# Attention and FFN block on one core: a new model for the order of TensorE's and ScalarE's work, transposes of o and of the FFN input by DMA, q and k in one padded tile

## The chip, the core and the metric

The program runs on one core of one Trainium2 chip. The core has a matrix engine (TensorE; its weight loads are listed apart), VectorE (DVE), ScalarE (ACT), GpSimd (POOL) and SyncE (SP), which here issues every DMA. The metric is the device time of one execution in microseconds. Lower is better.

## The reference

The input x has 2048 rows of 576 columns. A transformer block is computed: h = x + Attention(layernorm(x)), then out = h + FFN(layernorm(h)). Attention has 32 heads of 18 columns and works on four segments of 512 rows, with a memory M and its normalizer z that grow from segment to segment:

```python
for s in range(N):
    logits = jnp.einsum('bhqd,bhkd->bhqk', qs, ks) * scale + mask
    p = _softmax(logits, axis=-1)
    a_dot = jnp.einsum('bhqk,bhkd->bhqd', p, vs)
    pq = phi(qs)
    a_mem = (pq @ M) / (pq @ z + 1e-06)
    o = g * a_mem + (1.0 - g) * a_dot
    M = M + phi(ks).T @ vs
    z = z + phi(ks).sum(rows)
```

Here phi(t) is t + 1 above zero and exp(t) below, g is the sigmoid of beta for each head, the mask is causal within a segment, and o is multiplied by wo. The FFN is gelu(x w1 + b1) w2 + b2 with 4608 inner columns.

## The kernel before, in words

The work is cut into Python generators ("threads"), five kinds for each segment s of 512 rows (four tiles of 128):

- P (line 193): layernorm of x, TensorE transposes (`transposes5`, line 165) with a ScalarE copy out of PSUM, then q, k and v, each in two halves of five matmuls (`proj_half`, line 171). q and k go into tiles where each head's 18 columns are padded to 32 (`q_pad`, `k_pad`), and from there to memory (`qd`, `kd`, lines 232 and 238). For segments 0 to 2, phi(k) is then written over `k_pad` in place (line 245).
- M (line 253): phi(k) times v, added up in `MZacc`.
- A (line 283): attention, in eight groups of four heads. `fetch` (line 288) reads q and k of a group back from memory, transposed by two DMAs (lines 292 and 294). Two groups make five steps (STEPS, line 280), so a segment has 20: score matmuls into `st` (four PSUM banks, one buffer; line 372), Exp on ScalarE (line 376), the mask on GpSimd (line 378), and the products with v into `ox` (one buffer; line 346). `memory` adds the memory's part, `combine` normalizes and writes o into `o_nat`. phi(q) takes ScalarE, GpSimd and DVE (lines 301 to 306).
- B (line 407): TensorE transposes of o, times wo, plus x, layernorm (line 428), h to memory (`hd`), TensorE transposes of the normed h into `xn2T_s`.
- C (line 463): FFN1 in 36 chunks of five matmuls with 512 columns (lines 488 and 489), the copy to `hT` by DVE (line 490), a Gelu in place over twelve chunks at a time on ScalarE (line 495), so three for each segment; then FFN2, eight groups of 36 matmuls (line 511). The bias b1 is a 65th row of the last block of w1, loaded by a DMA of its own (line 475).

A loop at line 566 builds the order. Each generator yields a cost on TensorE and a delay; the loop keeps a clock of TensorE (and a rough one of ScalarE, `on_act`), takes the first thread of the list that is ready, in the order A, P and M, B, C, and emits its next piece. `manual_schedule` keeps that order for TensorE and ScalarE. `hT` lies in the space of the early tiles, so C0 comes after P3. What a thread has to wait for is in its `add` call:

```python
add(f"A{s}", thread_A(s), f"P{s}", *([f"M{s - 1}", f"A{s - 1}"] if s else []), *([f"B{s - 2}"] if s > 1 else []))
add(f"B{s}", thread_B(s), f"A{s}", *([f"B{s - 1}"] if s else []), *([f"C{s - 3}"] if s > 2 else []))
add(f"C{s}", thread_C(s), f"B{s}", f"P{NSEG - 1}", *([f"C{s - 1}"] if s else []))
```

All other PSUM work shares three banks (`bank`, line 162), taken in turn.

Of the kernel before, what the change touches and what calls it, by code (L numbers as in the profile page):

```python
# [16 lines left out]
def kernel(  # L17
# [15 lines left out]
    nc = tc.nc  # L33
# [21 lines left out]
    xtp = ctx.enter_context(tc.tile_pool(name="xtp", bufs=2))  # L55
    xn2Tp = ctx.enter_context(tc.tile_pool(name="xn2Tp", bufs=3))
# [6 lines left out]
    w1pool = ctx.enter_context(tc.tile_pool(name="w1pool", bufs=3))  # L63
# [11 lines left out]
    x_pre = []  # L75
    wts = {}

    def load_w(nm, W, wt):
        nc.sync.dma_start(out=wt[:, 0:4, :], in_=W[0:512, :].rearrange("(k p) n -> p k n", p=P))
        nc.sync.dma_start(out=wt[0:64, 4, :], in_=W[512:576, :])  # L80
        nc.gpsimd.memset(wt[64:KTAIL, 4, :], 0.0)
        wts[nm] = wt

    for tl in range(TPS):
        xt = xpool.tile([P, D], BF16, tag="x", name="xt")
        nc.sync.dma_start(out=xt[:], in_=x[tl * P:(tl + 1) * P, :])
# [12 lines left out]
    xn_bufs = [early([P, XW], f"xn{j}") for j in range(2)]
# [30 lines left out]
    b1_row = B_b1.rearrange("(o f) -> o f", o=1)  # L130
# [12 lines left out]
    qd = [tc.dram_tile([L, H * 32], BF16, name=f"qd{j}") for j in range(NSEG)]  # L143
    kd = [tc.dram_tile([L, H * 32], BF16, name=f"kd{j}") for j in range(NSEG)]
    hd = tc.dram_tile([S, D], F32, name="hd")
    big = {}
    w2_sb = const.tile([P, NF, D], BF16, name="w2_sb")
    w2v = B_w2.rearrange("(f p) d -> p f d", p=P)

    def layernorm(src, xn):  # L150
        stats = small.tile([P, 2, 6], F32, tag="stats", name="stats")
        for c in range(2):
# [4 lines left out]
        nc.vector.tensor_scalar(out=rstd[:], in0=mv[:, 1:2], scalar1=EPS, scalar2=None, op0=ALU.add)  # L157
        nc.gpsimd.tensor_tensor(out=rstd[:], in0=rstd[:], in1=mhalf[:], op=ALU.pow)  # L158
        nc.vector.tensor_scalar(out=xn[:, 0:D], in0=src, scalar1=mv[:, 0:1], scalar2=rstd[:],  # L159
                                op0=ALU.subtract, op1=ALU.mult)  # L160

    def bank(name):
        return psC.tile([P, 512], F32, tag="c", name=name)

    def transposes5(src):
        pt = bank("ps_t")[:].bitcast(BF16)[:, 0:KT * P].rearrange("p (k q) -> p k q", q=P)
        for k in range(KT):
            nc.tensor.transpose(out=pt[:, k, :], in_=src[:, k * P:(k + 1) * P], identity=ident[:])  # L168
        return pt

    def proj_half(xT_t, wt, hf, name):
        ps = bank(name)
        for k in range(4):
            nc.tensor.matmul(out=ps[:, 0:HALF], lhsT=xT_t[:, k, :], rhs=wt[:, k, hf * HALF:(hf + 1) * HALF],  # L174
                             start=(k == 0), stop=False)
        nc.tensor.matmul(out=ps[:, 0:HALF], lhsT=xT_t[0:KTAIL, 4, :], rhs=wt[0:KTAIL, 4, hf * HALF:(hf + 1) * HALF],
                         start=False, stop=True)
        return ps[:, 0:HALF]
# [4 lines left out]
    class Clock:  # L183
        pe = 0.0
        act = 0.0

    clk = Clock()

    def on_act(cost):
        clk.act = max(clk.act, clk.pe) + cost  # L190
        return clk.act

    def thread_P(s):
        va = v_augs[s]
        xns, xnTs = {}, {}

        def load(tl):
            t = s * TPS + tl
            if s == 0:
                xt = x_pre[tl]  # L200
            else:
                xt = xpool.tile([P, D], BF16, tag="x", name="xt")
                nc.sync.dma_start(out=xt[:], in_=x[t * P:(t + 1) * P, :])
            xns[tl] = xn_bufs[tl % 2]
            layernorm(xt[:], xns[tl])

        def flip(tl):
            pt = transposes5(xns[tl])
            xnTs[tl] = xtp.tile([P, KT, P], BF16, tag="xnT", name="xnT_t")
            nc.scalar.copy(out=xnTs[tl][:], in_=pt)  # L210
            on_act(0.65)

        load(0)
        load(1)
        yield 0.0, 3.0
        flip(0)
        yield 0.28, 0.0
# [398 lines left out]
```

## Time and profile before

| what | value |
|---|---|
| median of 3 runs | 573.83 us (571.47 to 577.94) |
| profiled execution | 574.9 us, its span 573.2 us |
| mean granted TensorE clock | 0.932 of full speed |
| TensorE, DVE, ScalarE, GpSimd busy | 500.0, 302.2, 292.3, 148.6 us |
| DMA | 63.42 MB, mean 111 GB/s |

All times of the rows below are microseconds from the start of the span. A row of a table of windows has the window, its length, the busy time of TensorE, its weight loads, DVE, ScalarE and GpSimd (in brackets how many instructions began there), then the granted TensorE clock as a share of full speed, the DMA share and GB/s. In a list of groups the columns are busy time and mean time of one in ns, then the idle time before them and what ended most of it. In the chain each row is start, length, and what ran or what was waited for. A letter q behind an engine's name (SPq) is its instruction queue.

### The profile page before, as it was taken

Reading aid. Unit: us, or ns where it says so; the run is one execution under the profiler, and the core shown is the slowest. Engines: PE = TensorE matmul, PEld = TensorE weight load, DVE = VectorE, ACT = ScalarE, POOL = GpSimd, SP = SyncE. Lnnn points to the kernel's source line nnn. Section 1 sums busy time; section 2 is a strip of 40 time slices with the busy share of each in tenths; the row PEclk is TensorE's granted clock in tenths of the full one; section 3 lists DMA queues with packets and bytes.
Section 4 is the critical chain, followed back from the end, with each engine's and each line's share of the span. In section 5 each row is a group of like instructions: output and inputs, shape, how many; then the busy total and the mean of one; then the engine's idle time right before and its main releaser. Section 6 shows DMA issues by size and latency. Waiting matters only on the chain.

```text
span 573.2 us, 11399 instructions
## 1 busy us (share of the span) xinstructions
PE 500.0 (87%) x4709; PEld 317.4 (55%) x4736; DVE 302.2 (53%) x722; ACT 292.3 (51%) x223; POOL 148.6 (26%) x236
## 2 busy tenths in 40 slices
PE   3756869878768997979989979799999999999997
PEld 2544656656544444647755534477754477644675
DVE  5384755656766766824437867144486611366200
ACT  2224666846766784776654768955415330033300
POOL 5013543514364303513332531132131000000000
PEclk9886977978977997979999999999999999999999
DMA  8977633515343442512233543211235421242020
GB/s 256 352 214 197 184 78 93 146 55 131 115 114 91 121 134 82 171 33 71 81 70 112 145 131 125 70 41 33 63 106 160 149 73 32 79 149 84 0 63 22
DMA packets 80347, 63.42 MB, mean 111 GB/s; under 512 B 38148, under 2 KB 72104, under 8 KB 80296
## 3 DMA queue, kind: packets, MB, share of 16 engines
q1 hardware_dynamic: 80296, 62.70, 37.2%
q8 instruction: 37, 0.61, 0.4%
q14 instruction: 14, 0.11, 0.1%
HBM read 38.83 MB, written 15.47 MB: 95 GB/s over the span
## 4 chain that ended last, share of the span: by engine, by line
PE 65%; ACT 12%; DVE 8%; DMA 5%; issue 4%; POOL 3%; SPq 2%; ACTq 0%; DVEq 0%; POOLq 0%
ACT hT L495 6%; ACT pt L376 4%; PE ox L346 4%; PE st L372 3%; PE ps_k L174 2%; DMA xt<-in_A_x_dram 2%; PE ps_q L174 2%; PE ps_v L174 2%; DVE stats L153 2%; PE ps_o L174 1%; POOL pt L378 1%; PE ps_t L168 1%; DMA kd_212<-k_pad_132 1%; POOL rstd L158 1%; DVE hT L490 1%
## 5 line engine op out<-in xcount | busy, mean ns | idle before, releaser
L376 ACT ACTIVATE pt<-st 128x2048 bf16<-128x2048 f32 x80 | 150.1, 1876 | 82.6 <-PE st L372 70.7
L511 PEld LDWEIGHTS <-hT 128*128 128x128 bf16 x1152 | 110.2, 99 | 34.2 <-issue 4.6
L378 POOL TENSOR_SCALAR_AFFINE_SELECT pt<-pt 128x512 bf16<-128x512 bf16 x128 | 82.8, 664 | 139.2 <-ACT pt L376 139.1
L495 ACT ACTIVATE hT<-hT 128x6144 bf16<-128x6144 bf16 x12 | 63.9, 5324 | 75.1 <-DVE hT L490 75.0
L488 PEld LDWEIGHTS <-w1g 128*128 128x128 bf16 x576 | 53.8, 98 | 67.6 <-issue 11.8
L346 PEld LDWEIGHTS <-pt 128*128 128x128 bf16 x1280 | 43.3, 98 | 21.9 <-POOL pt L378 11.2
L174 PEld LDWEIGHTS <-xnT_t 128*128 128x128 bf16 x384 | 38.0, 106 | 27.7 <-issue 13.7
L372 PE MATMUL st<-QT,KTt 32*128 32x384 bf16 (+3 forms) x512 | 34.4, 323 | 19.1 <-ACT pt L376 16.5
L306 DVE SCALAR_TENSOR_TENSOR pq<-e_g,r_g 128x512 bf16<-128x512 bf16 x24 | 17.6, 734 | 30.1 <-ACT e_g L301 25.3
L372 PEld LDWEIGHTS <-KTt 32*128 32x128 bf16 x512 | 10.0, 93 | 41.2 <-issue 37.6
L304 POOL TENSOR_SCALAR r_g<-QT 128x512 bf16<-128x512 bf16 x24 | 14.7, 612 | 60.3 <-DVE pq L306 54.8
L158 POOL TENSOR_TENSOR rstd<-rstd,mhalf 128x1 f32<-128x1 f32 x32 | 17.6, 558 | 48.2 <-DVE rstd L157 44.5
L174 PE MATMUL ps_k<-wt_k,xnT_t 128*128 128x288 bf16 x128 | 24.9, 326 | 4.8 <-ACT xnT_t L210 2.9
L174 PE MATMUL ps_o<-wt_o,oT_t 128*128 128x288 bf16 x128 | 22.7, 306 | 5.3 <-ACT oT_t L416 2.6
L174 PE MATMUL ps_q<-wt_q,xnT_t 128*128 128x288 bf16 x128 | 25.2, 330 | 2.3 <-ACT xnT_t L210 1.2
L489 PEld LDWEIGHTS <-w1g 65*128 65x128 bf16 x144 | 14.1, 98 | 17.6 <-issue 0.7
L174 PE MATMUL ps_v<-wt_v,xnT_t 128*128 128x288 bf16 x128 | 22.1, 299 | 2.1 <-DVE k_pad_133 L236 1.6
L434 ACT COPY xn2T_s<-ps_t 128x640 bf16<-128x640 bf16 x16 | 10.9, 690 | 23.6 <-PE ps_t L168 23.6
L429 POOL TENSOR_TENSOR h_t<-h_t,b_bc 128x576 f32<-128x576 f32 x16 | 20.4, 1274 | 8.9 <-DVE xn_1_155 L159 4.6
L416 ACT COPY oT_t<-ps_t 128x640 bf16<-128x640 bf16 x16 | 10.6, 691 | 20.6 <-PE ps_t L168 20.6
L153 DVE BATCH_NORM_STATS2 stats<-xt 128x6 f32<-128x288 bf16 x32 | 13.3, 440 | 12.4 <-DMA xt<-in_A_x_dram 12.3
L174 PEld LDWEIGHTS <-oT_t 128*128 128x128 bf16 x128 | 12.6, 103 | 11.0 <-issue 3.5
(864 smaller groups left out, 927.6 us busy)
## 6 DMA issues: line engine op xcount, KB each, us to landing
w1g<-in_B_w_dram SPq DMA_DIRECT2D x36, 512.0 KB
w_sb<-in_B_w_dram SPq DMA_DIRECT2D x4, 1296.0 KB
hd<-h_t SPq DMA_DIRECT2D x16, 288.0 KB
hc<-hd SPq DMA_DIRECT2D x16, 288.0 KB
xt<-in_A_x_dram SPq DMA_DIRECT2D x16, 144.0 KB
w1g<-in_B_w_dram SPq DMA_DIRECT2D x36, 64.0 KB
out_dram<-ot SPq DMA_DIRECT2D x16, 144.0 KB
wt_q<-in_A_wq_dram SPq DMA_DIRECT2D x1, 576.0 KB
```

Source lines behind the costliest of these rows:

```text
L153: nc.vector.bn_stats(out=stats[:, c, :], in_=src[:, c * HALF:(c + 1) * HALF])
L158: nc.gpsimd.tensor_tensor(out=rstd[:], in0=rstd[:], in1=mhalf[:], op=ALU.pow)
L174: nc.tensor.matmul(out=ps[:, 0:HALF], lhsT=xT_t[:, k, :], rhs=wt[:, k, hf * HALF:(hf + 1) * HALF], start=(k == 0), stop=False)
L306: nc.vector.scalar_tensor_tensor(out=pq[:], in0=e_g[:], scalar=1.0, in1=r_g[:], op0=ALU.min, op1=ALU.add)
L346: nc.tensor.matmul(out=banks[g][:, qt, i, :], lhsT=src, rhs=va[kt][:, 4 * g + i, :], start=fresh, stop=False, skip_group_check=True)
L372: nc.tensor.matmul(out=st[:, i, off:off + n], lhsT=kts[g][rows, kt * P:(kt + 1) * P], rhs=qts[g][rows, kt * P:L], start=True, stop=True, t ...
L376: nc.scalar.activation(out=pt_[:], in_=st[:], func=ACT.Exp, scale=scale)
L378: nc.gpsimd.affine_select(out=pt_[:, :, off:off + P], in_=pt_[:, :, off:off + P], pattern=[[0, 4], [1, P]], compare_op=ALU.is_ge, fill=0.0 ...
L429: nc.gpsimd.tensor_tensor(out=h_t[:], in0=h_t[:], in1=b2_bc[:], op=ALU.add)
L488: nc.tensor.matmul(out=ps[:], lhsT=w1g[:, k, j * P:(j + 1) * P], rhs=xn2T_s[:, k, :], start=(k == 0), stop=False)
L495: nc.scalar.activation(out=hT[:, f0:f1, :], in_=hT[:, f0:f1, :], func=ACT.Gelu_apprx_tanh)
L511: nc.tensor.matmul(out=ps[:, 0:HALF], lhsT=hT[:, f, tl * P:(tl + 1) * P], rhs=w2_sb[:, f, hf * HALF:(hf + 1) * HALF], start=(f == 0), stop ...
```

## The change

The loop now keeps a time for each of TensorE, ScalarE, DVE, GpSimd and SP (`free`, `on`) and for each of the three shared PSUM banks (`banks_free`). A thread yields a time at which it is ready and the number of banks that it needs, and is taken when both are there. The list is now in the order B, A, then X, P, M, then C. Layernorm and transposes of x become a thread X of their own. In the code:

```diff
+    free = dict(pe=0.0, act=0.0, dve=0.0, pool=0.0, sp=0.0)
+    def on(eng, cost, *after):
+        end = max([free[eng]] + [a + SEM for a in after]) + cost
+        free[eng] = end
+        return end
...
+    def flip_dma(dst, src, t0, cost=1.25):
+        nc.sync.dma_start_transpose(out=dst, in_=src)
+        return on("sp", cost, t0) + 2.0
+    def copy(out, in_, t0, ca, cd):
+        if max(free["act"], t0) + ca < max(free["dve"], t0) + cd:
+            nc.scalar.copy(out=out, in_=in_)
+            return on("act", ca, t0)
+        nc.vector.tensor_copy(out=out, in_=in_)
+        return on("dve", cd, t0)
...
     for s in range(NSEG):
-        add(f"A{s}", thread_A(s), f"P{s}", *([f"M{s - 1}", f"A{s - 1}"] if s else []), *([f"B{s - 2}"] if s > 1 else []))
+        add(f"B{s}", thread_B(s), f"A{s}", *([f"B{s - 1}"] if s else []), *([f"C{s - 2}:0"] if s > 1 else []))
+    for s in range(NSEG):
+        add(f"A{s}", thread_A(s), f"P{s}", *([f"M{s - 1}", f"A{s - 1}"] if s else []), *([f"B{s - 1}"] if s > 1 else []))
+    for s in range(NSEG):
+        add(f"X{s}", thread_X(s), *([f"X{s - 1}", f"P{s - 1}:0"] if s else []), *([f"P{s - 3}"] if s > 2 else []))
+        add(f"P{s}", thread_P(s), *([f"P{s - 1}"] if s else []), *([f"M{s - 2}"] if s > 1 else []))
...
+            def at(t):
+                return max(t.ready, bank_at(t.banks))
+            pick = next((t for t in open_ if at(t) <= free["pe"] + 1e-6), None)
```

q and k of a tile go into one padded tile (two of them in turn), in the order k, q, then v, with one write to memory, and a group's q and k come back by one transposing DMA of 256 columns. phi(k) goes to five tiles of its own:

```diff
+    pads = [early([P, G, 2, 4, 32], f"qk_pad{j}") for j in range(2)]
+    fk_pads = [early([P, H, 32], f"fk_pad{j}") for j in range(NK)]
...
+        qk = alp.tile([P, 2, L], BF16, tag="qk", name="qk")
+        at = flip_dma(qk[:], qkd[s][:, g * 256:(g + 1) * 256], qk_at[s], 2.1)
```

o goes to memory in five chunks of 128 columns, each when the heads in it are done, and comes back transposed; so does the normed h. The TensorE transposes and ScalarE copies of both are gone (those of x stay):

```diff
+            for k in ready_chunks.get(g, []):
+                nc.sync.dma_start(out=od[s].rearrange("(t p) c -> p t c", p=P)[:, :, k * P:(k + 1) * P],
+                                  in_=o_nat[:, :, k * P:(k + 1) * P])
...
+                oT_at[s] = flip_dma(oTs[s][:, k:k + 1, :], od[s][:, k * P:(k + 1) * P], wr)
...
+        for k in range(KT):
+            x2_at[s] = flip_dma(x2T[:, k:k + 1, :], x2d[s][:, k * P:(k + 1) * P], wr)
```

In segments 1 to 3 the last step of the layernorm of x is done by GpSimd. The bias b1 is loaded once, transposed, and added when FFN1 leaves PSUM; once all of attention is done, ScalarE takes FFN1 out of PSUM with Gelu and bias in one instruction a chunk:

```diff
+                if f"A{NSEG - 1}" in done and not pend:
+                    nc.scalar.activation(out=hT[:, f, :], in_=ps[:], func=ACT.Gelu_apprx_tanh, bias=b1c[:, f:f + 1])
+                    act_at[f] = banks_free[b] = on("act", 0.65, t1)
+                    continue
+                nc.vector.tensor_scalar(out=hT[:, f, :], in0=ps[:], scalar1=b1c[:, f:f + 1], scalar2=None, op0=ALU.add)
```

FFN2 is emitted in pieces of six matmuls instead of eight or nine. w1 has three fixed buffers, w2 is loaded in six parts instead of four, most memsets move behind the first layernorm, and the first loads are x, wk, x, wq, wv.

## Rows read from the trace of the kernel before

**Rows 1.** The page, part 1: busy time, share, instructions of each engine.

```profile
PE 500.0 (87%) x4709; PEld 317.4 (55%) x4736; DVE 302.2 (53%) x722; ACT 292.3 (51%) x223; POOL 148.6 (26%) x236
```

**Rows 2.** Table of windows, cut at the stages of the program.

```profile
40.80:120.60 79.80, 63.41 (x802) 44.54 (x803) 46.34 (x129) 52.32 (x53) 32.59 (x51) 0.80 0.49 133
120.60:175.50 54.90, 41.60 (x509) 28.45 (x508) 35.19 (x96) 36.35 (x39) 23.33 (x34) 0.84 0.40 107
175.50:252.30 76.80, 68.22 (x592) 35.96 (x600) 49.25 (x105) 54.93 (x36) 23.07 (x34) 0.92 0.40 114
252.30:295.00 42.70, 42.70 (x545) 30.62 (x542) 17.22 (x47) 24.63 (x17) 15.73 (x25) 0.94 0.23 57
295.00:370.20 75.20, 64.50 (x573) 34.40 (x579) 47.76 (x101) 54.21 (x35) 21.93 (x32) 0.98 0.41 119
370.20:406.70 36.50, 36.50 (x478) 26.56 (x476) 14.36 (x40) 21.76 (x14) 11.29 (x19) 0.95 0.16 45
406.70:465.50 58.80, 57.15 (x354) 31.92 (x358) 36.41 (x70) 22.69 (x12) 8.49 (x10) 1.00 0.38 119
...
495.10:570.00 74.90, 74.21 (x464) 45.33 (x466) 28.69 (x45) 15.97 (x3) 0.00 (x0) 1.00 0.22 68
```

**Rows 3.** The chain that ended last, in order of time: segment 0, and the end.

```profile
16.11 6.82 DMA kd_212<-k_pad_132
23.06 0.77 DVE k_pad_132 L245
...
31.94 3.49 DMA qd_208<-q_pad_131
35.45 1.23 SPq L292
...
39.31 1.26 SPq L294
...
565.44 4.42 PE ps_f_7412 L511 x36
```

**Rows 4.** Groups of instructions, costliest first.

```profile
L376 ACT ACTIVATE pt<-st 128x2048 bf16<-128x2048 f32 x80 | 150.1, 1876 | 82.6 <-PE st L372 70.7 <-POOL pt L378 9.3 <-POOL r_g L304 2.5
...
L495 ACT ACTIVATE hT<-hT 128x6144 bf16<-128x6144 bf16 x12 | 63.9, 5324 | 75.1 <-DVE hT L490 75.0
...
L158 POOL TENSOR_TENSOR rstd<-rstd,mhalf 128x1 f32<-128x1 f32 x32 | 17.6, 558 | 48.2 <-DVE rstd L157 44.5 <-DMA xt_6252<-in_A_x_dram 3.6
...
L153 DVE BATCH_NORM_STATS2 stats<-h_t 128x6 f32<-128x288 f32 x32 | 14.1, 453 | 0.6
...
L495 ACT ACT_TABLE_LOAD x7 | 9.0, 1283 | 0.1
...
L159 DVE TENSOR_SCALAR xn_1_155<-h_t,mv,rstd 128x576 bf16<-128x576 f32 x8 | 5.2, 653 | 4.2 <-POOL rstd L158 4.2
```

**Rows 5.** TensorE's instructions in order of time: values, transposes, scores.

```profile
45.13 0.63 PE L346 MATMUL ox<-v_aug_0_138,pt 128*128 128x19 bf16 x16
...
123.15 0.56 PE L168 MATMUL ps_t<-ident,o_nat_156 128*128 128x128 bf16 x7 [2.04 <-DVE o_nat_156 L331]
...
127.81 0.39 PE L372 MATMUL st<-QT,KTt 32*128 32x512 bf16 x4
```

**Rows 6.** ScalarE's instructions in order of time, FFN2 of segment 0.

```profile
268.75 1.88 ACT L376 ACTIVATE pt<-st 128x2048 bf16<-128x2048 f32 x1 [1.57 <-PE st L372]
...
285.35 1.88 ACT L376 ACTIVATE pt<-st 128x2048 bf16<-128x2048 f32 x1 [1.57 <-PE st L372]
```

**Rows 7.** ScalarE's instructions in order of time, A1 up to the first FFN matmul.

```profile
128.32 1.88 ACT L376 ACTIVATE pt<-st 128x2048 bf16<-128x2048 f32 x1 [1.33 <-PE st L372]
...
174.45 1.88 ACT L376 ACTIVATE pt<-st 128x2048 bf16<-128x2048 f32 x1 [0.80 <-POOL pt L378]
```

**Rows 8.** Line 490, the copy of an FFN1 chunk out of PSUM (min/median/max ns).

```profile
L490 DVE CAST hT<-ps_f_2736 x1: 692/692/692, 179.7 to 179.7; 128x512 bf16<-128x512 f32 x1
```

**Rows 9.** Instructions in order of time, first 60 us, SP's queue.

```profile
9.98 1.77 SPq L563 DMA_DIRECT2D w_sb<-in_B_w_dram  x2
```

More of the change, by code (lines that the diff above doesn't have):

```diff
@@ L157, in layernorm @@
         nc.vector.tensor_scalar(out=rstd[:], in0=mv[:, 1:2], scalar1=EPS, scalar2=None, op0=ALU.add)
+        t1 = on("dve", 1.25, t0)
         nc.gpsimd.tensor_tensor(out=rstd[:], in0=rstd[:], in1=mhalf[:], op=ALU.pow)
[L159 to L169, printed above, removed]
@@ L171, in proj_half @@
-    def proj_half(xT_t, wt, hf, name):
-        ps = bank(name)
-        for k in range(4):
[L174 to L178, printed above, removed]
+        t1 = on("pool", 0.56, t1)
+        eng = nc.vector if apply == "dve" else nc.gpsimd
@@ L187, with thread_X, fetch, ask @@
[L187 to L191, printed above, removed]
+    xnTs, xn_at = {}, {}
+    def thread_X(s):
+        yield 0.0, 0
+        xnTs[s] = xTp.tile([P, KT, L], BF16, tag="xT", name="xnT")
+        xs = {}
+        def fetch(tl):
+            xs[tl] = x_pre[tl] if s == 0 else load_x(s * TPS + tl)
+            return dma(free["pe"], 2.5)
+        at = [4.0, 4.5, 7.0, 7.5] if s == 0 else [0.0] * TPS
+        def ask(tl):
+            if tl < TPS:
+                t1 = fetch(tl)
+                at[tl] = max(at[tl], t1)
+        ask(0)
+        ask(1)
+        for tl in range(TPS):
+            ask(tl + 2)
+            done = layernorm(xs[tl][:], xn_bufs[tl % 2], at[tl], "pool" if s else "dve")
+            if s == 0 and tl == 0:
+                make_identity(nc, ident[:])
+            yield done + SEM, 1
+            pt, j = bank("ps_t")
+            pt = pt[:].bitcast(BF16)[:, 0:KT * P].rearrange("p (k q) -> p k q", q=P)
+            for k in range(KT):
+                nc.tensor.transpose(out=pt[:, k, :], in_=xn_bufs[tl % 2][:, k * P:(k + 1) * P], identity=ident[:])
+            t1 = on_pe(0.3)
+            banks_free[j] = copy(xnTs[s][:, :, tl * P:(tl + 1) * P], pt, t1, 0.69, 0.8)
+            xn_at[(s, tl)] = banks_free[j]
+            if s == 0 and tl == 0:
+                pads_first()
+            yield 0.0, 0
@@ L193, in thread_P @@
+    qk_at = {}
     def thread_P(s):
         va = v_augs[s]
[L195 to L211, printed above, removed]
@@ L354, in thread_A, with drain @@
-        yield 0.0, 5.0
+                    combine(g, oxs[g], free["pe"])
+        yield qk_at[s], 0
+        fetch(s, 2)
         phi(0)
         phi(1)
-        prev, late, ready = None, [], 0.0
+        prev, late, st_at = None, [], 0.0
+        def drain(prev):
+            psi, pgp, todo, at = prev
+            if s and psi in (0, 3):
+                g = 2 * pgp + (psi == 3)
+                yield max(pq_at[g] + SEM, mem_at[s - 1] + SEM), 1
+                memory(g)
+            fresh = todo[0][0] not in oxs
+            yield max(at + SEM, ox_at[0] + SEM if fresh else 0.0), 0
+            values(todo)
+            if psi == 0:
+                flip_o()
@@ L569 @@
             if pick is None:
[L570 to L575 removed]
+                pick = min(open_, key=at)
+                free["pe"] = at(pick)
+            try:
+                pick.ready, pick.banks = next(pick.gen)
+                done.add(pick.name + ":0")
             except StopIteration:
[L577 removed]
+                threads.remove(pick)
```

456 lines of the change are left out of this document (233 added, 223 removed).

## The prediction

> **What bounds the kernel now.** I read the page's busy line first, then a table of windows cut at the events of the program, then the chain that ended last, and last the order of single instructions around the waits that the chain named.
>
> TensorE is busy 500 of 573.2 us [rows 1], and no other engine is above 302 us. So the question is where TensorE loses time. The table by stage [rows 2] answers it. Its cuts are: 9.4 first matmul, 40.8 first score matmul of segment 0, 120.6 first transpose of that segment's attention output o, 175.5 first FFN matmul, and from there the alternation of FFN1 and FFN2. In the last line, the last segment's FFN alone, TensorE is busy 74.21 of 74.9 us at clock 1.00: nothing is to be had there. In 40.8 to 175.5 it is busy 63.41 of 79.80 and 41.60 of 54.90 us, and at a granted clock of 0.80 and 0.84, that is, about a third or more of these stretches at the lower of its two levels (1.2 GHz) after gaps. This is the finding: for 175.5 us no FFN work exists. FFN needs B0 (output projection, layernorm, transposes of segment 0) and P3 (the last of the projections), and B0 comes late: A0 ends at 120.6 and B0 needs another 55 us, because its pieces stand behind A1 and P3 in the list of threads.
>
> After 175.5 the FFN fills TensorE, yet not fully: 68.22 of 76.80, 64.50 of 75.20, 57.15 of 58.80 and 74.21 of 74.90 us are busy, which leaves 21.6 us idle; and the clocks of 0.92, 0.94, 0.98 and 0.95 mean that 16, 12, 4 and 10% of these stretches ran at half speed, some 12.3, 5.1, 3.0 and 3.7 us, half of which, 12 us, is lost [rows 2]. Together 33.6 us.
>
> **The sum that I forecast.** The end is S, the time of the first FFN matmul, plus R, what TensorE still has to do after it, plus the tail. Before: S = 175.5, R = 570.0 - 175.5 = 394.5, tail 573.2 - 570.0 = 3.2.
>
> *Start of A0.* Before, it begins at 40.8. In the chain [rows 3] one write of k takes 6.82 us to land, and the operation that overwrites this same tile with phi(k) waits for it (23.06), then the scalar queue behind it, then TensorE. The change gives phi(k) tiles of its own, so this wait goes. It comes back in part: q and k share two padded tiles, so a tile's k copy waits for the write of two tiles ago; I take half the loss, some 1.5 of 3 us. Next, the fetch: the chain shows transposed loads at 1.23 to 1.26 us each, and A0 starts when four of them are through (35.45 to 40.6). After, one load brings q and k of a group. A load of twice the columns appears nowhere in the trace; it lies between 1.25 us (the issue is the cost) and 2.5 us (the bytes are), and I take 2.1, nearer the upper end since the shown loads move the same bytes in each instruction. That saves about 3 us net of the landing. Memsets behind the first square root and the order of weight loads may give another us or cost one. A0 starts at 36 (34 to 41).
>
> *A0.* It has 20 steps: scores, Exp of 2048 columns, mask, value products. The Exp takes 1.876 us [rows 4] and waits for its scores, since there is one score buffer: no step can be under 1.88 + 0.39 (score group, [rows 5]) = 2.3 us. Before, 79.8 us for A0 is 4.0 a step. Where only FFN2 pieces lie between, five steps from 268.75 to 285.35 took 3.3 each, the two phi operations included [rows 6]. The new order, which books each engine and bank, should hold 3.3 where the old one let copies of P stand before the Exp: 20 x 3.3 = 66, so A0 ends at 102 (82 to 121).
>
> *B0.* TensorE transposes and ScalarE copies go; o goes to memory and comes back transposed. New on the path: the write's landing, 3 us (3.49 and 6.82 in [rows 3]; o is written while little else moves), two transposed loads, 2.5, and landing, 1.5. The three earlier chunks lie behind A0's steps. Then four tiles of projection, add and layernorm. By [rows 4] a tile's statistics are 2 x 0.45, the power on GpSimd 0.56 and the scaling 0.65 us; with two adds and the small operations 3 us a tile, 12 in all. Then the write, 3, five loads, 6.3, and landing, 1.5. Sum 30 us (25 if loads overlap, 52 if B keeps the 54.9 us of before). B now heads the list, so A1 yields to it. S = 36 + 66 + 30 = 132.
>
> What must be done by then besides: P1 to P3 are 36 units of q, k or v tile projections. TensorE has 96 us for these, A0, and part of A1; before, it did them, A0 and most of B0 in 105 busy us, at the lower clock in part. It fits, barely; if P3 is late S moves with it.
>
> *R.* Transposes that go: 24 groups of five after 175.5. Seven in a row took 0.56 us [rows 5], with 0.22 for the latency of one, hence 0.057 each and 0.28 a group: -6.7 us. Steps that come on top: in the old order, 13 steps of A1 were through by 175.5 (first and last in [rows 7]); now A1 starts at 104 and by 132 has some 8. Five more steps, each 0.39 of scores and sixteen value products at (0.63 - 0.17)/15 = 0.031, 0.9 us: +4.5. Of the 33.6 us of idle and half clock I give half back, -17: a wait that is booked is filled with FFN pieces, but each FFN1 group still frees its bank by a DVE or ScalarE operation. That gives R = 394.5 - 6.7 + 4.5 - 17 = 375 (359 with all of it, 392 with none).
>
> *What costs nothing.* The bias moves from a row of the weights to the eviction: 0.692 us before [rows 8], with a scalar operand between 0.69 and, as bounded by twice that, 1.4; I take 0.7 since size and operands in PSUM are the same. It hides behind a chunk's TensorE time, (74.9 - 8 x 4.42)/36 = 1.1 us by [rows 2, 3]; at 1.4 it would be the bound, and cost 72 x 0.3 = 22 us in the two segments where DVE does it. In the last two ScalarE does Gelu straight from PSUM: 5.32/12 = 0.44 us a chunk in [rows 4], plus a start, under 1.1. Twelve layernorm scalings go to GpSimd: 0.65 us each on DVE, at most double on GpSimd, which is busy 32.59 of 79.80 us in A0 [rows 2]; off the path. SP loses 32 transposed loads and 36 bias rows, and gains 40 transposed loads of o and of the normed input, 36 writes, and 32 loads that may be twice as long: between 10 and 50 us more over the kernel, hidden so long as SP runs ahead of A by its two groups.
>
> The sum: 132 + 375 + 3.2 = 510 us of span. The profiled execution took 574.9 us for its span of 573.2, so 1.7 us lie around it: 512. It stands 1.1 us above the median of 573.83, so I predict 511.
>
> **Two rules against the trace.** The transposed loads [rows 3] run at 1.23 to 1.26 us each, one after the other. The Trainium skill (Advanced Engine Details and Errata, X-Bar Transpose (TRN2)) holds that transposing DMAs are as fast as regular ones. By that rule B0's seven loads would be nearly free and the sum, as an estimate, some 7 us less, 504; the trace disagrees, and I stay with the row.
>
> The first transposed load starts at 35.45, just when the write of q ends (31.94 + 3.49): the queue stood waiting. The Trainium skill (DMA: Bandwidth & Descriptors, Two DMAs through the same engine are not ordered) wants exactly this: the issuing engine waits for the first DMA before it issues the one that reads its result. The trace agrees. It speaks against the change, which adds such write-and-read pairs on SP: the second rival.
>
> **Rivals.**
>
> *One: the chain of A and B is the bound.* A2 now waits for B1 and A3 for B2, which the old list did not ask, and three Gelu batches per segment stand in ScalarE's queue before an Exp: 5.32 + 2 x 1.28 = 7.9 us each, six of them in C0 and C1 [rows 4]. The last FFN cannot start before 36 + 4 x 66 + 6 x 7.9 + 3 x 30 = 437, if all six delay A; then 74.9 + 3.2 + 1.7 follow: 517. With A at its old 4.0 a step 56 us more, 573, which counts Gelu twice if the old pace held some of it; without the 47 us it is 526. I take the middle of 517 and 573 for this rival, some 542. For it: the Exps stood 70.7 us idle until their scores came [rows 4]. Against: B first in the list.
>
> *Two, slower: SP's queue.* Every transposed load of o waits at SP's head for its write, and behind it stand the q and k loads of A and the weights of FFN1. Here A and FFN stop together and nothing fills. Price: if each of the 32 group loads comes late by t, 32 t is added to a chain at 517. From t = 1.8 us (56 us) it is slower than before; a landing of 6.82 [rows 3] at each of four waits a segment would give 3.4 us a group, 109 us: 626. For it: that landing was seen, while weights streamed. Against: o is written later, in stages with a DMA share of 0.16 to 0.41 [rows 2], and loads are asked two groups ahead.
>
> *Three: the order isn't what the model says.* Only TensorE and ScalarE keep the written order; a load of w2 that the program asks for after P0 stands at 9.98 [rows 9]. If DVE, GpSimd and SP reorder so that the bookings fail, S falls by little and nothing is won back: 160 + 392 + 5 - 1 = 556.
>
> *Four: nearly all is won back*: S = 122 by a shorter A0, R = 359, so 485.
>
> **How the numbers follow.** Forecast 0.60, rival one 0.20, two 0.06, three 0.06, four 0.08. The likeliest gives 511 us. The range, 484 to 556, holds rival four's 485 and rival three's 556, and leaves out rival two. About 1% is what a measurement of this kernel can tell from no change. Faster by over 1%: 0.90; within 1% (rival one or three stretched to 570): 0.04; slower: 0.06.
>
> **What would show it.** Right: first FFN matmul at 120 to 145; TensorE at clock 1.00 and over 95% busy from there; A0's Exps 3.3 us apart; no ps_t of o. Wrong: TensorE waiting on DMA of qk (rival two); the last FFN starting straight after B3 with TensorE idle before (one); first FFN matmul after 155.

## The result and the profile after

The changed kernel takes 547.26 us (544.81 to 550.29) against 573.51 us before on the same chip, a ratio of 0.9535 [0.9457, 0.9612]; measured once more on another chip (g2_after_again), 547.71 us and 0.9501 [0.9466, 0.9536]. It is faster, as forecast with 0.90, and inside the range; but the gain is 26 us, not 62. The profiled execution took 545.85 us for a span of 544.1.

Busy time after, on the page (to set beside [rows 1]):

```profile
PE 482.2 (89%) x4577; PEld 304.0 (56%) x4577; DVE 267.5 (49%) x628; ACT 297.8 (55%) x262; POOL 187.6 (34%) x265
```

TensorE is 17.8 us less busy for a span 29.1 us shorter; GpSimd is 39 us busier.

Windows of the changed kernel (columns as in [rows 2]). The cuts are its first score matmul, the last value matmuls of A0, its first FFN matmul, the first FFN chunk of segment 3 after the wait, and the end of TensorE's work; the last line joins the last two stretches:

```profile
42.70:114.20 71.50, 62.96 (x843) 45.97 (x843) 38.05 (x95) 54.87 (x67) 48.81 (x54) 0.92 0.70 192
114.20:150.20 36.00, 24.61 (x346) 16.36 (x343) 25.19 (x67) 24.00 (x23) 21.93 (x29) 0.80 0.67 171
150.20:465.20 315.00, 294.68 (x2730) 177.84 (x2728) 176.59 (x378) 175.13 (x96) 85.76 (x121) 0.96 0.49 122
465.20:540.80 75.60, 75.60 (x464) 45.57 (x461) 3.20 (x7) 24.75 (x36) 0.00 (x0) 0.97 0.22 64
150.20:540.80 390.60, 370.28 (x3192) 223.41 (x3189) 179.80 (x385) 199.87 (x132) 85.76 (x121) 0.96 0.44 111
```

The kernel before in the same cut, from its first FFN matmul to its end:

```profile
175.50:570.00 394.50, 372.88 (x3229) 228.36 (x3254) 196.91 (x415) 194.20 (x115) 80.51 (x117) 0.97 0.30 89
```

S, the first FFN matmul, came down from 175.5 to 150.2 (forecast 132). R, what follows it, came down by 3.9 us only. What is lost in R is the idle time plus half of the time in which TensorE was busy at 1.2 GHz. (The prediction took half of all time at that clock, which counts idle time at that clock one and a half times.) Before, TensorE was busy 22.6 us at that clock: 21.6 + 11.3 = 32.9 us lost. After, 23.6 us, most of them in 150.2 to 159.4, 398.3 to 405.1 and 463.1 to 470.0: 20.3 + 11.8 = 32.1. Next to nothing of the lost time was won back. A second profile of the changed kernel (g2_after_again) has its first FFN matmul at 153.6 and 30.3 us lost in R, so 3 us between two single profiles tell nothing.

The chain that ended last, in order of time, around S (start us, us, what):

```profile
33.18 2.33 POOL xn_107 L195
...
36.44 6.20 DMA qk<-qkd_172
42.63 0.05 issue
42.68 0.61 PE st L469 x4
...
119.43 3.98 DMA oT<-od_176
...
143.00 3.73 DMA qk<-qkd_173
146.73 0.02 issue
146.75 0.02 POOLq L364
146.77 0.11 issue
146.88 0.61 POOL r_g L364
147.49 1.05 POOL pt L477
148.54 0.05 issue
148.59 0.49 PE ox L428 x12
...
150.90 3.65 DMA qk<-qkd_173
154.56 0.02 issue
154.58 0.02 POOLq L364
154.60 0.11 issue
154.71 0.61 POOL r_g L364
155.32 0.60 POOL pt L477
155.92 0.05 issue
155.97 0.28 PE ox L428 x4
156.25 1.72 PE ps_f_2607 L556 x4
```

What SP did in those microseconds (its timeline):

```profile
143.00 1.29 SPq L202 DMA_TRANSPOSE qk<-qkd_173  x1
144.38 6.42 SPq L202 DMA_TRANSPOSE x2T<-x2d_180  x5
150.90 1.63 SPq L202 DMA_TRANSPOSE qk<-qkd_173  x1
```

Read the two together. A1's next q,k load stands behind B0's five loads of x2 and starts at 150.90. It lands at 154.55. GpSimd takes its work in order: it stands at `r_g`, which reads that load, and the mask of an Exp already done stands behind it. TensorE's value matmuls wait for that mask, and the second FFN chunk, whose input is there, stands behind them. So a queue of SP reaches TensorE through GpSimd, an engine that is 34% busy. The wait here is 1.06 us; the longest of this kind comes in A2, whose q,k load stands behind B1's loads of x2:

```profile
244.82 0.28 PE L428 MATMUL ox<-v_aug_0_142,pt 128*128 128x19 bf16 x4 [4.08 <-POOL pt L477]
```
```profile
POOL r_g L364 <- DMA qk<-qkd_174: 6.6, 2, 5.5
```

(The second row is from the list of waits: us in total, times, longest.) In R TensorE waits 6.2 us for masks, these two waits among them, and 5.4 us for loads of o and x2 to land.

Two groups of the new kernel that I had priced without a row:

```profile
L195 POOL TENSOR_SCALAR xn_107<-xt,mv,rstd 128x576 bf16<-128x576 bf16 x6 | 15.0, 2501 | 0.0
L195 POOL TENSOR_SCALAR xn_108<-xt,mv,rstd 128x576 bf16<-128x576 bf16 x6 | 14.7, 2448 | 0.6 <-PE ps_t L253 0.6
```

A layernorm scaling takes GpSimd 2.5 us; "at most double" of [rows 4] was 1.3.

### The profile page after: what moved, and what is told of

Same layout as the page of the kernel before. It is cut to its first block, busy times and chain, and to the rows that moved or that the text cites. A ratio compares the mean times of both kernels' runs of the same rounds, so it can differ in the third digit from the quotient of the medians.

```text
span 544.1 us, 11123 instructions
## 1 busy us (share of the span) xinstructions
PE 482.2 (89%) x4577; PEld 304.0 (56%) x4577; DVE 267.5 (49%) x628; ACT 297.8 (55%) x262; POOL 187.6 (34%) x265
## 4 chain that ended last, share of the span: by engine, by line
PE 56%; ACT 9%; DMA 9%; POOL 8%; DVE 7%; issue 7%; SPq 2%; ACTq 0%; POOLq 0%; DVEq 0%
ACT pt L474 6%; PE st L469 4%; DMA xt<-in_A_x_dram 3%; PE ox L428 3%; ACT hT L568 2%; POOL pt L477 2%; PE ps_k L217 2%; DVE stats L186 2%; POOL xn_107 L195 1%; PE ps_v L217 1%; POOL h_t L518 1%; POOL rstd L192 1%; SPq L202 1%; DMA qk<-qkd_173 1%; DMA qk<-qkd_172 1%
## 5 line engine op out<-in xcount | busy, mean ns | idle before, releaser
L477 POOL TENSOR_SCALAR_AFFINE_SELECT pt<-pt 128x512 bf16<-128x512 bf16 x128 | 85.6, 688 | 153.7 <-ACT pt L474 153.6
L568 ACT ACTIVATE hT<-hT 128x6144 bf16<-128x6144 bf16 x9 | 47.9, 5324 | 5.4 <-DVE hT L563 5.4
L469 PE MATMUL st<-qk 32*128 32x384 bf16 (+3 forms) x512 | 33.9, 319 | 17.1 <-ACT pt L474 11.2
L217 PEld LDWEIGHTS <-xnT 128*128 128x128 bf16 x384 | 36.6, 102 | 22.0 <-issue 9.8
L556 PEld LDWEIGHTS <-w1g_165 128*128 128x128 bf16 x192 | 18.1, 103 | 26.2 <-issue 11.8
L469 PEld LDWEIGHTS <-qk 32*128 32x128 bf16 x512 | 10.5, 93 | 37.4 <-issue 30.3
L364 POOL TENSOR_SCALAR r_g<-qk 128x512 bf16<-128x512 bf16 x24 | 16.0, 668 | 41.8 <-DVE pq L367 17.2
L556 PEld LDWEIGHTS <-w1g_166 128*128 128x128 bf16 x192 | 18.0, 99 | 21.3 <-issue 1.8
L556 PEld LDWEIGHTS <-w1g_167 128*128 128x128 bf16 x192 | 17.2, 97 | 19.5 <-issue 1.3
L217 PE MATMUL ps_k<-wt_k,xnT 128*128 128x288 bf16 x128 | 23.3, 311 | 2.8 <-ACT xnT L207 1.7
L217 PE MATMUL ps_v<-wt_v,xnT 128*128 128x288 bf16 x128 | 21.6, 295 | 2.9 <-DVE xnT L209 1.9
L217 PE MATMUL ps_q<-wt_q,xnT 128*128 128x288 bf16 x128 | 21.4, 292 | 1.6 <-ACT qk_pad_101 L207 1.6
L217 PE MATMUL ps_o<-wt_o,oT 128*128 128x288 bf16 x128 | 20.5, 285 | 0.4 <-DMA oT<-od_176 0.3
L513 DVE TENSOR_TENSOR h_t<-ps_o,xt 128x288 f32<-128x288 f32 x32 | 14.0, 443 | 12.4 <-PE ps_o L218 11.0
```

The source lines that it names most:

```text
L217: nc.tensor.matmul(out=ps[:, 0:HALF], lhsT=xT[:, k, ts], rhs=wt[:, k, cs], start=(k == 0), stop=False)
L364: nc.gpsimd.tensor_scalar(out=r_g[:], in0=qts[s, g], scalar1=BIG, scalar2=0.0, op0=ALU.min, op1=ALU.max)
L469: nc.tensor.matmul(out=st[:, i, off:off + n], lhsT=kts[s, g][rows, kt * P:(kt + 1) * P], rhs=qts[s, g][rows, kt * P:L], start=True, stop=True,
L477: nc.gpsimd.affine_select(out=pt_[:, :, off:off + P], in_=pt_[:, :, off:off + P], pattern=[[0, 4], [1, P]], compare_op=ALU.is_ge, fill=0.0 ...
L556: nc.tensor.matmul(out=ps[:], lhsT=w1g[:, k, j * P:(j + 1) * P], rhs=x2T[:, k, :], start=(k == 0), stop=False)
L568: nc.scalar.activation(out=hT[:, f0:f + 1, :], in_=hT[:, f0:f + 1, :], func=ACT.Gelu_apprx_tanh)
```

## The experiments

All ratios are to the kernel before, run beside each on the same chip. "The changed kernel" is at 0.9535, or 0.9501 when run again.

| run | what differs from the changed kernel | us | ratio |
|---|---|---|---|
| g2_after_again | nothing | 547.71 | 0.9501 [0.9466, 0.9536] |
| e1_ln_on_dve | scalings back on DVE | 540.53 | 0.9404 [0.9367, 0.9442] |
| e2_ln_pool_booked | scalings booked at 2.4 us | 549.98 | 0.9573 [0.9537, 0.9608] |
| e3_x2_one_load | x2 in one load | 558.78 | 0.9717 [0.9679, 0.9755] |
| e4_A_not_after_B | A not after B, two pt tiles | 568.51 | 0.9890 [0.9856, 0.9925] |
| e5_before_B_first | kernel before, B first | 567.88 | 0.9856 [0.9808, 0.9905] |
| e6_w2_after_first_mask | w2 held back | 543.15 | 0.9424 [0.9378, 0.9471] |
| e7_x2_on_TensorE | x2 on TensorE | 546.59 | 0.9483 [0.9435, 0.9530] |
| e8_both_on_TensorE | x2 and o on TensorE | 530.39 | 0.9214 [0.9157, 0.9271] |
| f1_both_TensorE_ln_dve | e8 + e1 | 526.85 | 0.9168 [0.9130, 0.9205] |
| f2_f1_and_w2_late | e8 + e1 + e6 | 523.62 | 0.9119 [0.9078, 0.9161] |
| f3_o_on_TensorE | o on TensorE | 543.73 | 0.9459 [0.9397, 0.9521] |
| f4_both_TensorE_A_free | e8, A not after B | 549.39 | 0.9566 [0.9518, 0.9615] |
| g1c_both_TensorE_pt2 | e8, two pt tiles | 557.30 | 0.9700 [0.9639, 0.9762] |
| g1_idle_round_trips | g1c + trips nobody reads | 562.10 | 0.9772 [0.9719, 0.9825] |
| h1_both_TensorE_again | e8 again | 531.42 | 0.9237 [0.9191, 0.9283] |
| h2_idle_round_trips_pt3 | h1 + trips nobody reads | 539.87 | 0.9374 [0.9333, 0.9415] |

**GpSimd's scalings.** e1 and e2:

```diff
-            done = layernorm(xs[tl][:], xn_bufs[tl % 2], at[tl], "pool" if s else "dve")
+            done = layernorm(xs[tl][:], xn_bufs[tl % 2], at[tl], "dve")
```
```diff
-        return on(apply, 0.55, t1)
+        return on(apply, 0.55 if apply == "dve" else 2.4, t1)
```

> Edit: the last step of the layernorm of x is done by DVE in every segment, and booked as such (0.55 us), nothing else. In the profile of the changed kernel the twelve that GpSimd does take 2.29 to 2.90 us each where 0.55 is booked, and the masks of A0 and the phi(k) work stand behind them. Theory 'GpSimd price': masks come on time, A0 runs at some 3.3 us a step in place of 3.6, the first FFN matmul comes 5 to 9 us earlier, and the median falls by 4 to 9 us, from some 547 to 538 to 543. Rival 'hidden': GpSimd has slack (34% busy), DVE gets 12 x 0.6 us more, the median stays within 2 us.

> Edit: GpSimd keeps the last step of the layernorm of x in segments 1 to 3, but the model books 2.4 us for it in place of 0.55, so only the order changes. Theory 'wrong booking': what costs is that masks and transposes are emitted for a time at which GpSimd is still at the layernorm, TensorE waits in order; with the booking right, at least half of the gain of the run with DVE comes, 3 to 5 us. Theory 'price': GpSimd still spends 12 x 2.4 = 29 us in 20 to 105 us, beside the masks; at most 2 us are gained.

e1 wins 7 us by the medians, its first FFN matmul at 145.4 rather than 150.2. e2, with the scalings on GpSimd and booked right, wins nothing. So it is the duration on GpSimd that costs, not that the model books it too short.

**One load for x2, and A freed from B.** e3 and e4:

```diff
-        for k in range(KT):
-            x2_at[s] = flip_dma(x2T[:, k:k + 1, :], x2d[s][:, k * P:(k + 1) * P], wr)
+        x2_at[s] = flip_dma(x2T[:], x2d[s][:, :], wr)
```
```diff
-    oTp = ctx.enter_context(tc.tile_pool(name="oTp", bufs=1))
+    oTp = ctx.enter_context(tc.tile_pool(name="oTp", bufs=2))
-    ptpool = ctx.enter_context(tc.tile_pool(name="ptpool", bufs=3))
+    ptpool = ctx.enter_context(tc.tile_pool(name="ptpool", bufs=2))
...
-        add(f"A{s}", thread_A(s), f"P{s}", *([f"M{s - 1}", f"A{s - 1}"] if s else []), *([f"B{s - 1}"] if s > 1 else []))
+        add(f"A{s}", thread_A(s), f"P{s}", *([f"M{s - 1}", f"A{s - 1}"] if s else []), *([f"B{s - 2}"] if s > 1 else []))
```

(e4 also moves b1's rows into an output tile, for room.)

> Edit: the normed FFN input of a segment comes back by one transposing DMA of 640 columns in place of five of 128; booked once at 1.25 us. In the changed kernel a load of 256 columns holds SP's queue for 1.24 to 1.46 us (median), as one of 128 does (1.25). Theory 'price per load': one load of 640 holds SP for 1.3 to 2 us in place of 6.4, B ends 4 to 5 us earlier each time, q and k of A1 no longer stand behind it at 144 to 151, first FFN matmul some 4 us and the last FFN some 4 us earlier: median 4 to 7 us lower, 540 to 543. Rival 'price per byte': the load lands after 5 to 7 us as five did, nothing changes beyond 2 us.

> Edit: A of segment s waits for B of s-2, as before the change, not of s-1; for that the transposed o gets two buffers, and room is made by two buffers in place of three for the exponentials and by putting the rows of b1 into an output tile. Theory 'chain of A and B': in the changed kernel Exp stands still for 17 us before A2 and 28 us before A3 and the last FFN starts at 465 straight after B3, with TensorE idle and at half clock for some 7 us; now A3 ends 30 to 45 us earlier, the last FFN no longer waits for B3, and the median falls by 5 to 10 us. Rival 'TensorE does the same work and loses the same in each step of A': the stalls move with A, the median stays within 3 us.

e3 is some 11 us slower than the changed kernel, which neither theory had. Its tile x2T (min/median/max ns; then what TensorE waited for, us and times):

```profile
L202 SPq DMA_TRANSPOSE x2T<-x2d x4: 2876/2926/3027, 145.4 to 471.0; - x4
its engine sat idle before it (us, times) until:
  DMA x2T<-x2d: 15.9, 4
...
DMA to landing us min/median/max: 4.9/5.0/6.6
```

SP's time for x2 did fall, from 6.4 to 2.9 us a segment. But the model books the load at 1.25 us and 2.0 to landing, and it takes 4.9 us or more from issue. TensorE keeps the written order, so it stood 15.9 us in four waits, each at the head of a segment's FFN. The changed kernel waits 4.6 us for x2's loads, and the difference is the loss of 11. What the one load is worth with the right booking was not run. e4 is 21 us slower, but its loss can't be put down to A: it also gave up a pt tile, and g1c below shows what that does.

**B's place in the list, without the rest.** e5 moves the four `add(f"B{s}", ...)` lines of the kernel before to the head.

> The kernel before, with nothing changed but the place of the four B threads, which go to the head of the list. Theory 'priority': most of what the change won before the first FFN matmul (175.5 to 156 us) is B's place alone. Then the first FFN matmul falls from 175.5 to about 155 and the time by 15 to 20 us, to 554 to 559. Theory 'bookings': without booked engines and banks B's place does nothing, since TensorE then stands in order before B's waits; 571 to 577.

Between the two theories: 8 us. The first FFN matmul came at 164.0 rather than 175.5, and 4.5 us of that were given back after it. The other 18 us of the change's gain need more than B's place.

**w2 held back.**

```diff
+                if s == 0 and gp == 0 and si == 0:
+                    nc.gpsimd.tensor_copy(out=gate[:], in_=pt_[:, 0, 0:1])
...
+            nc.gpsimd.tensor_copy(out=w2_sb[:, c * 6, 0:1], in_=gate[:])
             nc.sync.dma_start(out=w2_sb[:, c * 6:(c + 1) * 6, :], in_=w2v[:, c * 6:(c + 1) * 6, :])
```

> The changed kernel with the six loads of w2 held until the first mask of A0 (GpSimd writes one column of each part, from a tile that it copies out of the first masked tile). Theory 'traffic': the 2.54 us wait of tile 3's k copy and the 6.2 us from issue to landing of the first q,k load come from w2's stream. Then the first score matmul falls from 42.7 to 37 to 39 us and the time by 3 to 6 us. Theory 'own write': they are the price of a write and a transposed load of the same rows, whatever else moves; first score at 42 to 43.5, time within 2 us of the changed kernel's ratio 0.9535.

The time fell by 4 to 5 us, as 'traffic' said, though its interval meets that of g2_after_again; the first score matmul moved only from 42.7 to 41.5, so the way there isn't the one expected. In f2, where DVE does the scalings as well, it does come at 37.34, with 0.36 us of wait left where the changed kernel has 5.1:

```profile
37.34 0.40 PE L472 MATMUL st<-qk 32*128 32x512 bf16 x4 [0.36 <-DMA qk<-qkd]
```

**The transposes back on TensorE.** e7 does x2, f3 does o, e8 both. These three, and all runs built on e8, also claim the two FFN2 banks of a segment's first pair together; that wasn't run by itself. Where B had a write and five loads, it has for each tile

```diff
+            yield at[tl] + SEM, 1
+            pt, j = bank("ps_t2")
...
+            for k in range(KT):
+                nc.tensor.transpose(out=pt[:, k, :], in_=xn2_bufs[tl % 2][:, k * P:(k + 1) * P], identity=ident[:])
+            banks_free[j] = copy(x2T[:, :, tl * P:(tl + 1) * P], pt, on_pe(0.3), 0.69, 0.8)
```

> The changed kernel with the normed FFN input transposed on TensorE again, in all four segments (16 groups of five transposes and 16 copies more, 16 writes and 20 transposed loads fewer); o still goes by DMA. Both FFN2 accumulators of a segment's first pair claim their banks together, which leaves the order of the changed kernel as it is. Theory 'B sets S, TensorE has room': the stretch from B0's last layernorm to the first whole FFN1 group, 14 us, shrinks to 4, and so do the three later ones; the first FFN matmul runs at 143 to 147 and the time falls by 6 to 12 us, to a ratio of 0.933 to 0.943. Theory 'TensorE's work is the bound': 16 x 0.28 = 4.5 us more of TensorE, nothing gained; ratio 0.958 to 0.965.

> The changed kernel with o alone transposed on TensorE (no od); x2 stays with the DMA. The half that e7 left out. Theory 'o's half costs': B waits for a write and five loads of o after each A, and A waits for B, so o makes most of the 17 us between the changed kernel and e8; ratio 0.925 to 0.935. Theory 'either way stays a round trip through memory': one of the two left is enough to hold the chain; ratio 0.943 to 0.953, as e7.

> As e7, and o transposed on TensorE too: no od, no x2d, 32 groups of five transposes in all on TensorE, with their copies. Theory 'B sets S, TensorE has room': another 4 us off B0's start, but P3 may set the first FFN matmul then; ratio 0.925 to 0.94. Theory 'TensorE's work is the bound': 32 x 0.28 = 9 us more; ratio 0.965 to 0.975.

Each half alone moves the time by less than the intervals can tell; both together win 16 to 17 us. One of the two trips left is enough to keep nearly all of the loss. The second theory of f3 said so; e7 came out between its two. In the traces a half moves the loss and doesn't remove it: e7 has its first FFN matmul at 143.8, as its first theory said, and then R is 398.9; f3 has it at 156.4, after a wait of 6.85 us for a mask behind a late q,k load, and R is 384.9. In e7 GpSimd waits only 5.6 us for q,k loads, yet TensorE stands at the new transposes until DVE has scaled (us, times, longest):

```profile
PE ps_t L508 <- DVE xn L195: 11.0, 9, 3.3
```

In e8 this is 1.1 us. So the queue isn't the whole of it; where a piece stands in TensorE's order counts as well.

**Queue or path.** g1 and h2 put the trips back beside e8's kernel, with nobody waiting for them; TensorE's and ScalarE's orders stay. g1 needed room for a spare tile, so it has a control, g1c. h2 loads into the other segment's o tile and into oT when each is free:

```diff
+            for k in ready_chunks.get(g, []):
+                nc.sync.dma_start(out=od[s].rearrange("(t p) c -> p t c", p=P)[:, :, k * P:(k + 1) * P],
+                                  in_=o_nat[:, :, k * P:(k + 1) * P])
+                flips.append((k, 0.0))
...
+                nc.sync.dma_start_transpose(out=spare[:, k:k + 1, :], in_=od[s][:, k * P:(k + 1) * P])
...
+            for k in range(KT):
+                nc.sync.dma_start_transpose(out=oTs[s][:, k:k + 1, :], in_=x2d[s][:, k * P:(k + 1) * P])
```

> The control for the next run: e8_both_on_TensorE with two pt tiles instead of three, and b1's rows in one of the output tiles, which frees 4.3 kB a partition. Order on TensorE and ScalarE as in e8. If the third pt tile is worth nothing: ratio 0.918 to 0.926. If it is worth something (the mask of one step and the Exp of the next but one then meet), 0.93 or more, and part of e4's loss was this.

> The control, with the round trips of o and x2 put back beside it for nothing: the od and x2d writes and the 40 transposed loads are issued where the changed kernel issues them, into a spare tile that nobody reads, and aren't booked, so that TensorE's and ScalarE's order is that of the control. Theory 'queue': the loads' time on SP (40 x 1.25 us) and the q,k loads and weights that stand behind them, or the bytes, cost what e8 won: 10 us or more above the control, ratio higher by 0.017 to 0.03, and GpSimd waits 15 us or more for q,k loads. Theory 'path': what costs is that B and the next A wait for the trip; then the spare trips cost under 3 us, ratio higher by less than 0.006.

> e8_both_on_TensorE once more, as the control of the next run on the same chip, with three pt tiles: ratio 0.916 to 0.927.

> h1 with the round trips of o and x2 beside it for nothing, and no buffer taken: the 36 writes and 40 transposed loads are issued where the changed kernel issues them; o's loads go to the other segment's o tile, free until the next A, x2's to the oT tile when B has read it; TensorE's and ScalarE's orders are those of h1. Theory 'queue': SP's 40 x 1.25 us and what stands behind them cost most of the 17 us: ratio higher than h1's by 0.018 to 0.03. Theory 'path': what costs is that B, and A behind it, wait for the trip; ratio higher by at most 0.008. By the run with two pt tiles (+0.007, its interval as wide as that) I give 'path' 3 to 1.

The control came out 27 us slower than e8, by a tile that I took for a detail. The group of the Exps in g1c, with 34.0 us of waits for value matmuls, and then in h1, where there are none:

```profile
L476 ACT ACTIVATE pt<-st 128x2048 bf16<-128x2048 f32 x80 | 150.3, 1879 | 94.6 <-PE st L471 56.0 <-PE ox L430 34.0 <-POOL pt L479 4.6
```
```profile
L476 ACT ACTIVATE pt<-st 128x2048 bf16<-128x2048 f32 x80 | 150.4, 1879 | 64.8 <-PE st L471 55.1 <-POOL pt L479 9.5
```

With two pt tiles an Exp waits until TensorE has read the tile of two steps ago. So g1's +4.8 us belongs to another kernel, and h2 was run. It stands 8.5 us above h1 by the medians, 0.0137 by the ratios: half of the loss, more than 'path' allows and less than 'queue' asks for. The waits of GpSimd for q,k loads (us, times, longest), h1:

```profile
POOL r_g L364 <- DMA qk<-qkd: 4.2, 5, 2.2
```

and h2:

```profile
POOL r_g L364 <- DMA qk<-qkd: 14.8, 7, 8.7
```

The changed kernel has 20.0 us of these, g1 35.6. R of h1, then of h2:

```profile
145.80:525.80 380.00, 368.52 (x3344) 229.48 (x3371) 187.17 (x401) 216.06 (x153) 87.89 (x124) 0.99 0.33 94
```
```profile
148.60:535.60 387.00, 370.24 (x3344) 229.89 (x3372) 186.23 (x401) 216.13 (x153) 88.62 (x125) 0.98 0.43 114
```

Lost in R, counted as above: h1 11.5 + 3.4 = 14.9 us, h2 16.8 + 5.5 = 22.3, the changed kernel 32.1, the kernel before 32.9. The rest of R is TensorE's work at full clock: 365.1 us in h1, 364.7 in h2, 358.5 in the changed kernel. So the DMA transposes take 6.6 us of work from TensorE, as much as was booked for them, and bring 17.2 us of idle and half clock.

h2's 7.4 us above h1 are one wait, here as TensorE and then as DVE shows it, with the lower clock in 154.8 to 161.6 behind it:

```profile
157.47 1.87 PE L601 MATMUL ps_f<-x2T,w1g 128*128 128x512 bf16 x4 [5.74 <-DVE hT L608]
```
```profile
DVE hT L608 <- DMA qkd<-qk_pad: 5.6, 1, 5.6
```

`hT` lies in the space of the early tiles, so DVE's first copy into it waits for P3's last write out of a padded tile. SP issues that write at 152.96, behind the five loads of x2 that nobody reads; in h1 it does so at 144.15. GpSimd's wait of 8.7 us ends inside this one, at 155.08, so the mask behind it would have held TensorE for a part of it too; elsewhere in R GpSimd's waits cost TensorE nothing (1.0 us for masks in h1 and in h2). In the changed kernel P3's last write goes out at 122.80, before the loads of x2, and TensorE's waits are the 6.2 us for masks. So h2 shows that loads which nobody reads cost by standing in SP's queue, but by another wait than the changed kernel's; it also moves more bytes (114 GB/s against 94), which wasn't separated. How the 17.2 us of the changed kernel divide into the queue, B's waits for the trips and the other order of TensorE that comes with e8 was not separated.

**A freed from B, without touching a buffer.** f4 is e8 with e4's last line.

> e8_both_on_TensorE with A2 waiting for B0 rather than B1, and A3 for B1 rather than B2 (the two o tiles allow it; no buffer is changed, as in e4 three of them were). Theory 'chain': the wait of A for B is what holds the end; ratio 0.905 to 0.915. Theory 'supply': a segment's A early only takes FFN work away from later A and B, whose gaps then stand empty; 10 to 20 us slower than e8, ratio 0.938 to 0.955, with TensorE's gaps in A3.

'Supply' fits: 19 us slower, 6 of them before the first FFN matmul (150.9 against 144.8 in e8). The start of segment 3's last Exps in f4, then in h1:

```profile
366.95 1.88 ACT L476 ACTIVATE pt<-st 128x2048 bf16<-128x2048 f32 x1 [0.98 <-PE st L471]
```
```profile
414.65 1.88 ACT L476 ACTIVATE pt<-st 128x2048 bf16<-128x2048 f32 x1
```

Attention is through 48 us earlier, and the end is later. Two windows of f4 show where it went:

```profile
280.00:320.00 40.00, 33.02 (x339) 18.84 (x339) 30.14 (x71) 28.60 (x21) 18.38 (x25) 0.91 0.50 123
320.00:360.00 40.00, 32.57 (x352) 19.14 (x355) 21.21 (x47) 33.71 (x18) 9.55 (x16) 0.91 0.25 67
```

14.4 us of these 80 are idle, and 3.5 more are lost to the lower clock, while A3 runs close behind A2; h1 is idle for 2.1 us of the same 80. That A2 and A3 lack FFN work between them is how I read it; no run shows it by itself.

**Two edits on top of e8.** f1 is e8 with e1's edit, f2 is f1 with e6's.

> e8_both_on_TensorE (ratio 0.9214) with the twelve layernorm scalings of segments 1 to 3 on VectorE again, as in e1. Theory 'the two add': GpSimd's 2.45 us each are on the way to P3 and to B0's power, whatever transposes x2 and o, so the 6 to 7 us of e1 are won again: ratio 0.908 to 0.913. Theory 'same gap': e1 and e8 filled the same gap ahead of the first FFN matmul; ratio 0.918 to 0.924.

> f1 with w2's loads held until A0's first mask, as in e6. Theory 'traffic': another 3 to 5 us, won before the first FFN matmul; ratio 0.006 to 0.009 below f1's. Theory 'nothing': e6's distance from the changed kernel (0.9424 against 0.9535, measured on two chips) came from elsewhere or from the chip; within 0.003 of f1.

Each adds 3 to 4 us, less than alone and between its two theories, with intervals that overlap its neighbour's. f2, at 523.62 us, is 9% faster than the kernel before and 4% faster than the changed one.

## Why the prediction was wrong, point by point

The sum said 132 + 375 + 3.2. The trace has 150.2 + 390.6 + 3.3.

*S, 18.2 us late, in three terms.* "A0 starts at 36": 42.7. The k copy behind its own write was there, 2.54 us where 1.5 were booked; what was left out is the 2.3 to 2.9 us scalings on GpSimd and w2's stream. Without the first A0 starts at 40.5 (e1), without the second at 41.5 (e6), without both at 37.3 (f2). "20 x 3.3 = 66": 71.5. The step of 3.3 was read where only FFN2 pieces lay between [rows 6]; here P1 to P3 had to fit as well. "It fits, barely" was the warning, but TensorE wasn't full: 62.96 of 71.5 us busy, at clock 0.92, are 57.5 us of work at full speed. GpSimd's scalings are part of it again: from the first Exp of A0 to the end of its twentieth e8 takes 68.6 us and f1, with the scalings on DVE, 64.6. "Sum 30 us" for B0: 36.0, with A1's q,k loads and GpSimd's masks in one another's way, as the chain shows. In f2 the first FFN matmul comes at 139.2, so 11 of the 18 us are gone with the trips, the scalings and w2's stream; for the other 7 no run shows a cause.

*R, 15.6 us too long.* "Of the 33.6 us of idle and half clock I give half back, -17": 0.8 came back. This is the step that failed most, and the reason is another step: "SP loses 32 transposed loads and gains 40 ..., hidden so long as SP runs ahead of A by its two groups". It isn't hidden: A1's and A2's q,k loads stand behind loads of x2, and TensorE behind them. With the trips off the path and off the queue, h1 does win back 32.9 - 14.9 = 18.0, which is the 17 of the forecast; that half was the right share is luck, since no row gave it. With the transposes on TensorE the forecast's R would be 375 + 6.7 = 382, and h1 has 380.0, f2 381.6. So the DMA transposes, booked as a saving of 6.7 us in R and otherwise at nothing, cost 17.2 there. Where nobody reads them (h2) they cost 8.5 us; the share of the queue in the changed kernel stays open. The other terms of R came out: work without losses of 358.5 us, where 394.5 - 33.6 - 6.7 + 4.5 = 358.7 was forecast.

*"At most double on GpSimd; off the path."* Four times DVE's 0.6 us, and on the path: 7 us (e1). The reason given, that GpSimd is busy less than half of A0, looks at its share and not at who is queued behind an instruction.

*Right:* the bias at the copy out of PSUM, 0.75 us on DVE for a booked 0.7, and Gelu from PSUM, 0.69 us, both under a chunk's 1.1; five B loads at 6.4 for a booked 6.3; the last FFN, 75.60 of 75.6 us busy.

*256-column loads,* booked at 2.1 between 1.25 and 2.5: they hold SP 1.24 to 1.46 us in the median, so the lower bound was right. The Trainium skill (Advanced Engine Details and Errata, X-Bar Transpose (TRN2)) says that transposing DMAs are as fast as regular ones. For the time on SP the trace disagrees again: a transposed load of 128 KB of x2 holds it 1.25 us, a regular load of 144 KB of x 0.35 us in the median. From issue to landing they are closer, 2.9 and 2.3 us in the median.

*The rivals.* Rival one gave 542 (the middle of 517 and 573 is 545), nearest to the result. One of its signs was there: the last FFN starts straight after B3, with 3.5 us of waits for x2's loads. But its mechanism falls in e8's kernel: freeing A from B makes that slower (f4). In the changed kernel itself it was tried only together with the loss of a pt tile (e4). Rival two, SP's queue, is a mechanism that is there, at 8.5 us in h2 rather than the 56 that it needed to decide; it reaches TensorE through GpSimd's order and DVE's. Rival three was not tested by itself; e8 wins with the order of SP, DVE and GpSimd as it is.

## What to carry to other kernels

When a transfer or an operation is moved to an engine with time to spare, ask what stands behind it in that engine's queue, and who waits for that: here SP delayed a load, GpSimd stood at the load's reader, and TensorE stood at GpSimd's next mask. A price that no row shows is best bounded by an instruction of the same operands, not by the same engine's other work. And an edit of several parts is worth undoing part by part: without the DMA transposes the change is worth some 45 us here (576.25 to 530.39, 576.37 to 531.42 again), and they gave 17 of it back. Take a control for every buffer that an experiment gives up.

## What the hardware showed that I had not expected

GpSimd's scaling with two per-partition operands takes 2.29 to 2.90 us for 576 bf16 columns, 4 to 5 ns a column; the same instruction with two constants, `r_g`, takes 0.61 for 512, 1.2 ns a column, and DVE does the scaling in 0.42 to 0.81 (e1), 0.7 to 1.4 ns a column. The Trainium skill (GPSIMD Engine Reference, 4.1 Engine selection) holds operations with one input on GpSimd to be roughly at line rate: the constant form agrees, the per-partition form doesn't. The two differ in what they compute as well (min and max against subtract and multiply), so that the operands are the reason isn't shown.

A transposed load holds SP some 1.25 us whether it brings 128 or 256 columns of 512 rows (medians of 1.14 to 1.26 and 1.24 to 1.46), and 2.9 us for 640 (e3); it lands 2.5 to 5.6 us after issue for 128 columns and 4.9 to 6.6 for 640. Five loads of 128 hold SP 6.4 us, and in segment 3 the last of them lands 8.0 us after the first is issued (456.6 to 464.6). So one wide load is cheaper for the queue and lands no later than the last of five, but nothing can start on a part of it.
